# Last keys by pair of visits or one by one, the last rows' order of products, and when weights are converted

## The chip, the cores and the metric

The kernel runs on one core of a Trainium2 chip. The metric is device time in microseconds from start to end of one launch; a kernel's time is the median over its runs. The engines of the core are TensorE (PE; its weight loads are PEld), VectorE (DVE), ScalarE (ACT), GpSimd (POOL) and SyncE (SP), which issues nearly all DMAs.

## The reference

Attention with normalized queries and keys, then a feed-forward network with a squared ReLU. Eight batches, 12 heads, 448 rows, head size 64; the network takes 3584 rows of 768, with 2048 hidden columns.

```python
q_n, k_n = (rmsnorm(q, g_q), rmsnorm(k, g_k))
scores = scale * np.matmul(q_n, k_n.transpose(0, 1, 3, 2))
attn = np.exp(scores - np.max(scores, axis=-1, keepdims=True))
attn = attn / (np.sum(attn, axis=-1, keepdims=True) + 1e-09)
x = np.matmul(attn, v)             # (B,H,S,D), then to (B*S, H*D)
h = np.maximum(x @ w_in, 0.0)
out = h * h @ w_out
```

q, k and v are float32; w_in and w_out come as 64-bit floats and are made into float32 on the chip.

## The kernel before

**Pairs and visits.** Two heads make a pair; there are 48 pairs, numbered i, six for each batch. A pair has 448 keys: three tiles of 128 (slots 0, 1, 2) and 64 last keys (slot NJ = 3). The last keys of an even pair and of the odd pair after it share one tile: the even pair's in partitions 0 to 63, the odd one's in 64 to 127 (`key_of`). A visit to pair i computes its scores (L405), takes the exponentials (L413, into tiles wT with 8 buffers), and multiplies the values of pair i - 1 (`attend`, L490), so values come one visit late. The products of the values gather in PSUM bank 4 from batch 2 on. Pairs up to 24 have two visits each, later ones (`whole`) one.

**Units.** The network's rows come in four units of two batches. A unit of `ffn` has four blocks. A block has first products (14 products, `first_products`, L733: half a block's cost) and second products (`second_products`, L785 and L814). Both matrix products are done by a scheme with seven products instead of eight, P1 to P7, whose left and right sides include sums of weight quarters ("forms") and whose results are added into four quarters of an output tile: c11, c12 in an upper row tile, c21, c22 in a lower. Three PSUM banks serve them by "roles": P1, P6 and P7 gather in role 0, P5 and P3 in role 1, P2 and P4 in role 2 in turn, and after each product VectorE adds the bank into the quarters (L855, L831). A product into a bank waits until the addition before it has read the bank.

**Interleaving.** TensorE's stream is written out by a generator with costs. A unit costs 2008, a block 502, a first product 18, a second product 10. `run(until)` emits products until the cost spent reaches a mark, then an attention visit is emitted, then more products. Unit one runs among the visits of pairs 12 to 24, units two and three among the visits of pairs 24 to 47, unit four has none. After each product, `run` also emits a sum of weight forms, the end of a conversion begun before, and a new conversion if its due time (the list `late`) has come.

**Conversion of weights.** Only unit one does it. There are 64 pieces of 128 x 384, 16 per block: four for each of two "in" tiles, then four for each of two "out" tiles. A piece is loaded (L896, L901; three buffers `words`), split by three ScalarE activations (L915 to L917), then joined by three VectorE steps (L928, L948, L952), spread over two due times. After the fourth piece of a tile come four sums of forms, by VectorE and GpSimd in turn (L974), and a store of the tile to DRAM, from which later units load it. Due times are spaced evenly before: sixteen to a block, from half a block on.

**Joint last keys.** From pair 24 on (`joint`), the last keys of an even pair and the odd one after it are multiplied at one time, in the odd visit, by `attend_both`: four products of 64 x 64 (L502). The odd pair's part goes to bank 0, is copied by ScalarE into a spare `words` buffer (L1189), and is added later in `finish` by VectorE (L609), after which GpSimd multiplies with the inverse of the denominators (L610). Other pairs take the other branch, one multiplication by VectorE (L612). Values of last keys lie in `lasts[0]` and `lasts[1]`, whose other 64 partitions are zero; `load_v` loads them (L355). In the joint case it loads both in the even visit, and `lasts[0]` once more in the odd one.

**Denominators.** In even visits `both_denominators` (L542) gives the sums of the two pairs before in bank 0; VectorE and GpSimd invert and spread them (L552 to L565) as tasks between later products.

**The end.** In the last block of the last unit, the rows of a tile are stored (L860) as soon as they are complete, 128 rows of 768 at a time, on SyncE's queue. The last tile (tt = 2) takes its products in SECOND_ORDER, so that P7, which goes into c21 and c22, comes last.

Of the kernel before, what the change touches and what calls it, by code (L numbers as in the profile page):

```python
# [13 lines left out]
F32 = mybir.dt.float32  # L14
# [3 lines left out]
ALU = mybir.AluOpType  # L18
# [3 lines left out]
P = 128  # L22


NJ = 3
# [198 lines left out]
def program(ctx, tc, rows, v, g, wide, ones, moe_w_in, moe_w_out, out, shift):  # L224

    nc = tc.nc

    B, H, S, D = v.shape
# [5 lines left out]
    HALF = DM // 2  # L234
    REST = S % P
    NT = S // P
    NBLK = 4
# [12 lines left out]
    lasts = [const.tile([P, 2, D], F32, name=f"lasts{n}") for n in range(2)]  # L250
# [15 lines left out]
    weights, sums, inverse, rests, xts, forms = {}, {}, {}, {}, {}, {}  # L266
    complete = deque()


# [4 lines left out]
    def whole(i):  # L274
        return i > 2 * 2 * NPAIR

    def joint(i):

        return whole(i - i % 2 + 1) and not shift

    def slots_of(i, n):

        return [m for m in (2 * n, 2 * n + 1) if m < NJ + 1 - i % 2]

    def values_of(i):

        if i % 2:
            return [0, 1, 2] if joint(i) else [NJ, 0, 1, 2]
        return [0, 1, 2, NJ]

    def key_of(i, m):
        return (i - i % 2, m) if m == NJ and not shift else (i, m)
# [51 lines left out]
    def load_v(i):  # L344
        b, c = pairs[i]
        values[i] = io.tile([P, NJ, 2, D], F32, name="vt", tag="vt")
        for e in range(2):
            nc.sync.dma_start(
                values[i][:, :, e],
                rows.in_chunks(i, v[b, 2 * c + e, 0 : NJ * P]),  # L350
            )
        for odd in range(2):
            if joint(i) != (i % 2 == odd) or joint(i) and i % 2 == 0:
                h = 2 * (c - i % 2 + odd)
                nc.sync.dma_start(  # L355
                    lasts[odd][ds(odd * D, D)],
                    v[b, h : h + 2, NJ * P : S].rearrange("h p d -> p h d"),
                )

    def rescale(i, x):  # L360
        rows.power(i, x)
# [63 lines left out]
    def add_up(i, e, m):  # L425
        if m == 1:
            sums[i, e] = new_sum(i)
            left = weights[(i, 0), e]
        else:
            left = sums[i, e]  # L430
        some = ds(i % 2 * LASTS, LASTS) if m == NJ else ds(0, P)
        nc.gpsimd.tensor_tensor(  # L432
            out=sums[i, e][some], in0=left[some], in1=weights[key_of(i, m), e][some], op=ALU.add
        )
        if joint(i) and i % 2 and m == NJ:
            del weights[key_of(i, m), e]

    def new_sum(i):

# [34 lines left out]
    def values_bank(i):  # L474
        return banks[4 + i % 2 if alone(i) else 4][:, 0:S]

    def attend(i, some):

        order = values_of(i)
        for n in some:
            m = order[n]
            if joint(i) and m == NJ:
                attend_both(i)
                continue
            mine = ds(i % 2 * LASTS, LASTS) if m == NJ and shift else ds(0, P)
            for e in range(2):
                nc.tensor.matmul(  # L490
                    values_bank(i)[ds(e * D, D), :],
                    lhsT=lasts[i % 2][mine, e, :] if m == NJ else values[i][:, m, e, :],
                    rhs=weights[key_of(i, m), e][mine], start=n == 0, stop=n == len(order) - 1,
                )

    def attend_both(i):

        other = banks[0][:, 0:S]
        for p in (i, i + 1):
            r = ds(p % 2 * LASTS, LASTS)  # L500
            for e in range(2):
                nc.tensor.matmul(  # L502
                    (other if p % 2 else values_bank(i))[ds(e * D, D), :],
                    lhsT=lasts[p % 2][r, e, :], rhs=weights[(i, NJ), e][r],
                    start=p > i, stop=True,
                )
        rests[i + 1] = new_words().bitcast(F32).rearrange("p n w -> p (n w)")[:, 0:S]

    def add_weights(i, some):

# [84 lines left out]
    def new_words():  # L595
        return ffn_p.tile([P, HALF, 2], U32, name="words", tag="words", bufs=3)
# [4 lines left out]
    def new_x():  # L601
        return ffn_p.tile([P, S], F32, name="xT", tag="xT", bufs=11 * NK - 1)

    def finish(i):

        b, c = pairs[i]
        xT = xts[b, c] = new_x()
        if joint(i):
            nc.vector.tensor_tensor(out=xT, in0=values_bank(i), in1=rests.pop(i), op=ALU.add)  # L609
            nc.gpsimd.tensor_tensor(out=xT, in0=xT, in1=inverse.pop(i), op=ALU.mult)  # L610
        else:
            nc.vector.tensor_tensor(out=xT, in0=values_bank(i), in1=inverse.pop(i), op=ALU.mult)  # L612
        leave(i)

    def leave(i):
# [81 lines left out]

    FIRST_ORDER = ["P1", "P5", "P2", "P6", "P3", "P4", "P7"]
    SECOND_ORDER = ["P1", "P2", "P5", "P6", "P4", "P3", "P7"]
    COST_IN, COST_OUT = 12 * NK // 2, 10  # L700
    COST = NF // 2 * 7 * COST_IN + NBLK * (NT * 7 + 4) * COST_OUT

# [68 lines left out]
    def second_products(u, blk, hid, sums_, accs):  # L771
# [34 lines left out]
        for tt in range(NT):  # L806
            upper_acc, lower_acc = accs[2 * tt], accs[2 * tt + 1]
            c11, c12 = [upper_acc[:, ts(h, HALF)] for h in range(2)]
            c21, c22 = [lower_acc[:, ts(h, HALF)] for h in range(2)]
            for name in SECOND_ORDER:  # L810
                role, first, left, right = PRODUCTS[name]
                ps = roles[role][:, 0:HALF]
                for t in range(2):
                    nc.tensor.matmul(  # L814
                        ps, lhsT=lefts[left][:, t, ts(tt, P)], rhs=w_sb[t][:, OUT.index(right), :],
                        start=first and t == 0, stop=t == 1,
                        skip_group_check=not first,
                    )
                if name == "P1":
                    add_to(c11, ps, blk == 0)  # L820
                elif name == "P5":
                    add_to(c22, ps, blk == 0)
                elif name == "P2":
                    add_to(c11, ps)
                elif name == "P6":
                    add_to(c12, ps, blk == 0)
                elif name == "P4":
                    if blk == 0:
                        nc.scalar.mul(c21, ps, -1.0)
                    else:  # L830
                        nc.vector.tensor_tensor(out=c21, in0=c21, in1=ps, op=ALU.subtract)  # L831
                elif name == "P3":
                    add_to(c12, ps)
                else:
                    add_to(c21, ps)
                    add_to(c22, ps)
                    to_store.append((tt, 1))
                if name == "P3":
                    to_store.append((tt, 0))
                if name in ("P2", "P4") and blk == NBLK - 1:  # L840
                    while to_store:
                        store_rows(*to_store.popleft())
                yield COST_OUT
            turn_roles(2, 0, 1)
# [6 lines left out]
    def add_to(acc, ps, first=False):  # L851
        if first:
            nc.scalar.copy(acc, ps)
        else:
            nc.vector.tensor_tensor(out=acc, in0=acc, in1=ps, op=ALU.add)  # L855
# [124 lines left out]
    def convert():  # L980
# [13 lines left out]
    block, tile_pieces = COST // NBLK, 4  # L994
    ahead = 4 * tile_pieces
    early = deque(2 + 2.4 * n for n in range(ahead + 1))
    every = block / ahead
    late = deque(
        block + 2 + every * (n - 2 * tile_pieces) for n in range(len(all_pieces) - ahead)
    )  # L1000

    load_weights(0)
    load_weights(1)
# [165 lines left out]
    def visit_whole(i):  # L1169
        run_tasks(len(tasks) + len(pool_tasks))  # L1170
        if i <= last and not shift:
            for m in slots_of(i, 0):
                score(i, m)
        if shift:
            attend_all(i - 1)
        else:
            for n in range(len(values_of(i - 1))):
# [100 lines left out]
```

## Time and profile before

| | us |
|---|---|
| median of three runs | 1426.91 |
| the three runs | 1429.25, 1426.91, 1426.72 |
| the profiled execution | 1429.25 |
| its span, first to last instruction | 1427.5 |
| PE busy | 1401.5 |
| DVE busy | 660.0 |
| ACT busy | 597.4 |
| POOL busy | 689.3 |
| first matmul of unit one, two, four (L733) | 137.4, 503.9, 1165.9 |

A matmul of float32 appears as two instructions, which are passes over the same columns. The profile gives each a length that overlaps the next one, so what a matmul costs is the distance from its start to the next start: 0.3755 us for 448 columns and 0.3225 us for 384. Products that use different halves or quarters of the array start a few nanoseconds apart and run at the same time.

### The profile page before, as it was taken

How to read it: one execution, taken by the hardware profiler on the slowest of the kernel's cores; microseconds unless marked ns; L12 is line 12 of the kernel's file. 1: busy time of each engine (PE TensorE's matmuls, PEld its weight loads, DVE VectorE, ACT ScalarE, POOL GpSimd, SP SyncE). 2: the span in 40 equal slices, each digit the busy share in tenths (PEclk: the TensorE clock that was granted, in tenths of full speed). 3: DMA queues.
4: the chain of work that ended last, by engine and by line, in shares of the span. 5: the costliest groups of instructions: out<-in, count | busy, mean ns of one | idle time of the engine just before them, and what ended most of it. 6: DMA issues, size and time to landing. Idle time of an engine off the chain costs nothing.

```text
span 1427.5 us, 15477 instructions
## 1 busy us (share of the span) xinstructions
PE 1401.5 (98%) x4932; PEld 677.4 (47%) x4932; DVE 660.0 (46%) x1233; ACT 597.4 (42%) x1126; POOL 689.3 (48%) x688
## 2 busy tenths in 40 slices
PE   7999999999999999999999999999999999999998
PEld 3333444444444445445454544445444455555554
DVE  5997365886777623324252453224233251132413
ACT  6874466647555254342424334442432303212130
POOL 5666654655556657356455566365462422021111
PEclk9999999999999999999999999999999999999999
DMA  5765336565667573453435454343622242213122
GB/s 139 195 193 151 67 96 196 157 197 164 197 183 218 160 209 94 127 138 99 138 78 172 122 182 126 74 149 87 185 71 89 95 153 79 111 55 127 39 89 80
DMA packets 311007, 188.51 MB, mean 132 GB/s; under 512 B 267524, under 2 KB 295044, under 8 KB 302724
## 3 DMA queue, kind: packets, MB, share of 16 engines
q1 hardware_dynamic: 310624, 187.36, 44.9%
q8 instruction: 41, 0.67, 0.2%
q14 instruction: 50, 0.41, 0.1%
q10 hardware_dynamic: 292, 0.07, 0.0%
HBM read 144.97 MB, written 42.40 MB: 131 GB/s over the span
## 4 chain that ended last, share of the span: by engine, by line
PE 91%; DVE 4%; issue 1%; SPq 1%; POOL 1%; ACT 1%; DMA 1%; DVEq 0%; POOLq 0%; ACTq 0%
PE bank L733 35%; PE bank L814 29%; PE bank L405 9%; PE bank L490 9%; PE bank L785 5%; PE bank L516 1%; PE bank L502 1%; PE bank L533 1%; PE bank L542 1%; SPq L157 1%; DVE acc L855 0%; DVE out_sb L974 0%; PE bank L370 0%; DVE out_sb L952 0%; DMA qk<-in_q_dram 0%
## 5 line engine op out<-in xcount | busy, mean ns | idle before, releaser
L733 PE MATMUL bank<-xT,in_sb 128*128 128x448 f32 x1344 | 515.4, 542 | 0.0
L733 PEld LDWEIGHTS bank<-xT,in_sb 128*128 128x128 f32 x1344 | 252.4, 190 | 260.4 <-issue 250.5
L855 DVE TENSOR_TENSOR acc<-acc,bank 128x384 f32<-128x384 f32 x324 | 173.8, 550 | 232.9 <-PE bank L814 183.7
L814 PE MATMUL bank<-out_sb,hid 128*128 128x384 f32 x768 | 266.6, 487 | 1.6 <-DVE acc L855 1.6
L753 DVE TENSOR_TENSOR hid<-bank,part 128x448 f32<-128x448 f32 x128 | 76.9, 622 | 331.9 <-PE bank L733 331.6
L413 ACT ACTIVATE wT<-bank,rr 128x448 f32<-128x448 f32 x288 | 161.5, 631 | 116.5 <-PE bank L405 85.2
L814 PE MATMUL bank<-out_sb,sums 128*128 128x384 f32 x576 | 204.0, 490 | 3.4 <-DVE acc L855 3.3
L814 PEld LDWEIGHTS bank<-out_sb,hid 128*128 128x128 f32 x768 | 145.4, 190 | 105.6 <-DVE acc L855 3.6
L202 POOL TENSOR_TENSOR rr<-ms,minus_half 128x8 f32<-128x8 f32 (+1 forms) x96 | 146.2, 1523 | 81.1 <-DVE ms L195 69.7
L769 POOL TENSOR_TENSOR sums<-hid 128x384 f32<-128x384 f32 x32 | 32.2, 1007 | 295.7 <-ACT hid L755 295.7
L405 PE MATMUL bank<-qT,kT 64*128 64x448 f32 (+1 forms) x768 | 164.5, 575 | 1.4 <-DVE qT L378 1.1
L754 ACT ACTIVATE hid<-hid 128x448 f32<-128x448 f32 x128 | 73.3, 572 | 197.1 <-DVE hid L753 197.1
L814 PEld LDWEIGHTS bank<-out_sb,sums 128*128 128x128 f32 x576 | 107.7, 190 | 88.2 <-DVE acc L855 8.4
L740 ACT COPY part<-bank 128x448 f32<-128x448 f32 x128 | 67.7, 529 | 170.9 <-PE bank L733 170.9
L432 POOL TENSOR_TENSOR sum<-sum,wT 128x448 f32<-128x448 f32 (+1 forms) x96 | 110.6, 1173 | 10.9 <-ACT wT L413 8.1
L405 PEld LDWEIGHTS bank<-qT,kT 64*128 64x128 f32 (+1 forms) x768 | 55.5, 174 | 104.6 <-issue 76.9
L490 PE MATMUL bank<-wT,vt 128*64 128x448 f32 x480 | 102.8, 549 | 0.0
L785 PE MATMUL bank<-out_sb,hid 128*128 128x384 f32 x256 | 85.6, 488 | 0.0
L432 POOL TENSOR_TENSOR sum<-wT 128x448 f32<-128x448 f32 x48 | 56.7, 1199 | 49.2 <-ACT wT L413 49.2
L554 POOL COPY few<-few 32x14 f32<-32x14 f32 x48 | 9.0, 188 | 144.9 <-DVE few L552 142.9
L192 DVE TENSOR_REDUCE ms<-squares 128x8 f32<-128x512 f32 (+1 forms) x68 | 41.8, 615 | 77.3 <-ACT squares L179 77.3
L755 ACT ACTIVATE hid<-hid 128x448 f32<-128x448 f32 x128 | 73.8, 577 | 4.1
(101 smaller groups left out, 1287.7 us busy)
## 6 DMA issues: line engine op xcount, KB each, us to landing
out_sb<-out_forms SPq DMA_DIRECT2D x24, 1536.0 KB, 9.4
in_sb<-in_forms SPq DMA_DIRECT2D x24, 1344.0 KB, 5.9
words<-in_moe_w_in_dram SPq DMA_DIRECT2D x32, 384.0 KB, 4.0
words<-in_moe_w_out_dram SPq DMA_DIRECT2D x32, 384.0 KB, 3.8
out_forms<-out_sb SPq DMA_DIRECT2D x8, 1536.0 KB, 7.1
in_forms<-in_sb SPq DMA_DIRECT2D x8, 1344.0 KB, 5.9
qk<-in_q_dram SPq DMA_DIRECT2D x96, 96.0 KB, 3.2
qk<-in_k_dram SPq DMA_DIRECT2D x96, 96.0 KB, 2.7
```

The lines of the kernel that those rows point to most:

```text
L202: self.nc.gpsimd.tensor_tensor(out=self.rr[i][:, x, 0 : self.count(i)], in0=ms, in1=self.minus_half.to_broadcast(list(ms.shape)), op=ALU.pow,)
L405: nc.tensor.matmul(sc[some], lhsT=turned[p, 1][r, keys], rhs=turned[p, 0][r, :], start=True, stop=True,)
L413: nc.scalar.activation(new_weights((i, m), e), sc, AF.Exp, scale=rows.rr[i][:, 1, 2 * m + e : 2 * m + e + 1],)
L432: nc.gpsimd.tensor_tensor(out=sums[i, e][some], in0=left[some], in1=weights[key_of(i, m), e][some], op=ALU.add)
L490: nc.tensor.matmul(values_bank(i)[ds(e * D, D), :], lhsT=lasts[i % 2][mine, e, :] if m == NJ else values[i][:, m, e, :], rhs=weights[key_o ...
L733: nc.tensor.matmul(ps, lhsT=w_sb[:, IN.index(left), c, :], rhs=forms[u, c][right], start=first and c == 0, stop=c == NK - 1, skip_group_ch ...
L753: nc.vector.tensor_tensor(out=dst, in0=left, in1=right, op=op)
L754: nc.scalar.activation(dst, dst, AF.Relu)
L755: nc.scalar.activation(dst, dst, AF.Square)
L785: nc.tensor.matmul(ps, lhsT=flat[a][:, t, ds(NT * P, P)], rhs=w_sb[t][:, 2 * a + half, :], start=(a, t) == parts[0], stop=(a, t) == parts[-1],
L814: nc.tensor.matmul(ps, lhsT=lefts[left][:, t, ts(tt, P)], rhs=w_sb[t][:, OUT.index(right), :], start=first and t == 0, stop=t == 1, skip_g ...
L855: nc.vector.tensor_tensor(out=acc, in0=acc, in1=ps, op=ALU.add)
```

## The change

It has three parts.

1. The joint product of the last keys goes, with its copy, its spare buffer, and its addition. Every pair's last keys are multiplied with the pair's other values, 128 partitions deep (the other half of `lasts` is zero): last in an even pair, first in an odd pair. `load_v` loads the pair's own last values only.
2. In the last row tile of the last block of the last unit, the products come in a new order, P1, P2, P6, P5, P7, P4, P3. The upper row tile is stored by halves: c11 after P2, c12 after P3; the lower one after P4.
3. The due times of the conversions change: of sixteen to a block, eight come 0.06 of a block apart from 0.4 on, and eight 0.055 apart from the start of the next block on.

```diff
     def values_of(i):
 
-        if i % 2:
-            return [0, 1, 2] if joint(i) else [NJ, 0, 1, 2]
-        return [0, 1, 2, NJ]
+        return [NJ, 0, 1, 2] if i % 2 else [0, 1, 2, NJ]
...
-        for odd in range(2):
-            if joint(i) != (i % 2 == odd) or joint(i) and i % 2 == 0:
-                h = 2 * (c - i % 2 + odd)
-                nc.sync.dma_start(
-                    lasts[odd][ds(odd * D, D)],
-                    v[b, h : h + 2, NJ * P : S].rearrange("h p d -> p h d"),
-                )
+        mine = ds(i % 2 * D, D)
+        nc.sync.dma_start(
+            lasts[i % 2][mine],
+            v[b, 2 * c : 2 * c + 2, NJ * P : S].rearrange("h p d -> p h d"),
+        )
...
-            if joint(i) and m == NJ:
-                attend_both(i)
-                continue
...
-        if joint(i):
-            nc.vector.tensor_tensor(out=xT, in0=values_bank(i), in1=rests.pop(i), op=ALU.add)
-            nc.gpsimd.tensor_tensor(out=xT, in0=xT, in1=inverse.pop(i), op=ALU.mult)
-        else:
-            nc.vector.tensor_tensor(out=xT, in0=values_bank(i), in1=inverse.pop(i), op=ALU.mult)
+        nc.vector.tensor_tensor(
+            out=xts[b, c], in0=values_bank(i), in1=inverse.pop(i), op=ALU.mult
+        )
...
     SECOND_ORDER = ["P1", "P2", "P5", "P6", "P4", "P3", "P7"]
+    LAST_ORDER = ["P1", "P2", "P6", "P5", "P7", "P4", "P3"]
...
+                if ends and name == "P4":
                     to_store.append((tt, 1))
-                if name == "P3":
-                    to_store.append((tt, 0))
+                if ends and name in ("P2", "P3"):
+                    half = int(name == "P3")
+                    nc.sync.dma_start(
+                        out[ds(2 * u * S + P * tt, P), ts(half, HALF)], [c11, c12][half]
+                    )
...
-    every = block / ahead
-    late = deque(
-        block + 2 + every * (n - 2 * tile_pieces) for n in range(len(all_pieces) - ahead)
-    )
+    def when(n):
+        step, n = divmod(n, ahead)
+        if n < ahead // 2:
+            return block * (step + 0.4 + 0.06 * n)
+        return block * (step + 1 + 0.055 * (n - ahead // 2)) + 2
+
+    late = deque(when(n) for n in range(len(all_pieces) - ahead))
...
-                nc.scalar.copy(rests[i], banks[0][:, 0:S])
                 xts[pairs[i - 1]] = new_x()
```

Here `ahead` is 16 and `block` is 502; `ends` is true in the last row tile of the last block of the last unit alone.

More of the change, by code (lines that the diff above doesn't have):

```diff
@@ L265, in program @@
     values, turned, through = {}, {}, {}
-    weights, sums, inverse, rests, xts, forms = {}, {}, {}, {}, {}, {}
+    weights, sums, inverse, xts, forms = {}, {}, {}, {}, {}
     complete = deque()
@@ L275, in whole @@
         return i > 2 * 2 * NPAIR
-    def joint(i):
-        return whole(i - i % 2 + 1) and not shift
     def slots_of(i, n):
@@ L434, in add_up @@
         )
-        if joint(i) and i % 2 and m == NJ:
-            del weights[key_of(i, m), e]
     def new_sum(i):
@@ L492, in attend @@
                     lhsT=lasts[i % 2][mine, e, :] if m == NJ else values[i][:, m, e, :],
-                    rhs=weights[key_of(i, m), e][mine], start=n == 0, stop=n == len(order) - 1,
+                    rhs=weights[key_of(i, m), e][mine], start=n == 0, stop=n == NJ,
                 )
[L496 to L505, printed above, removed]
-                )
-        rests[i + 1] = new_words().bitcast(F32).rearrange("p n w -> p (n w)")[:, 0:S]
     def add_weights(i, some):
@@ L606, in finish @@
         b, c = pairs[i]
-        xT = xts[b, c] = new_x()
-        if joint(i):
-            nc.vector.tensor_tensor(out=xT, in0=values_bank(i), in1=rests.pop(i), op=ALU.add)
-            nc.gpsimd.tensor_tensor(out=xT, in0=xT, in1=inverse.pop(i), op=ALU.mult)
-        else:
-            nc.vector.tensor_tensor(out=xT, in0=values_bank(i), in1=inverse.pop(i), op=ALU.mult)
+        xts[b, c] = new_x()
+        nc.vector.tensor_tensor(
+            out=xts[b, c], in0=values_bank(i), in1=inverse.pop(i), op=ALU.mult
+        )
         leave(i)
@@ L809, in second_products @@
             c21, c22 = [lower_acc[:, ts(h, HALF)] for h in range(2)]
-            for name in SECOND_ORDER:
+            ends = final and blk == NBLK - 1 and tt == NT - 1
+            for name in LAST_ORDER if ends else SECOND_ORDER:
                 role, first, left, right = PRODUCTS[name]
@@ L836, in second_products @@
                     add_to(c22, ps)
-                    to_store.append((tt, 1))
-                if name == "P3":
-                    to_store.append((tt, 0))
+                    if not ends:
+                        to_store.append((tt, 1))
+                if name == "P3" and not ends:
+                    to_store.append((tt, 0))
+                if ends and name == "P4":
+                    to_store.append((tt, 1))
+                if ends and name in ("P2", "P3"):
[3 more added lines that the diff above has]
+                    )
                 if name in ("P2", "P4") and blk == NBLK - 1:
@@ L996, in program @@
     early = deque(2 + 2.4 * n for n in range(ahead + 1))
-    every = block / ahead
-    late = deque(
-        block + 2 + every * (n - 2 * tile_pieces) for n in range(len(all_pieces) - ahead)
-    )
+    def when(n):
[4 more added lines that the diff above has]
+    late = deque(when(n) for n in range(len(all_pieces) - ahead))
     load_weights(0)
@@ L1176, in visit_whole @@
         else:
-            for n in range(len(values_of(i - 1))):
+            for n in range(NJ + 1):
                 attend(i - 1, (n,))
```

## The prediction

> **What bounds the kernel.** I first read the page's busy shares, to see whether one engine sets the time.
>
> ```profile
> span 1427.5 us, 15477 instructions
> ...
> PE 1401.5 (98%) x4932; PEld 677.4 (47%) x4932; DVE 660.0 (46%) x1233; ACT 597.4 (42%) x1126; POOL 689.3 (48%) x688
> ```
>
> TensorE does, and the page's row of granted clocks is at its top digit in all 40 slices. So an edit costs what it adds to TensorE's stream or to a gap in it; work on another engine counts only where TensorE waits for it. I then read the stretches of each weight block, one row each: the first unit's four second-product stages start at 185.6, 274.0, 366.2 and 456.1 us. Columns: length, then busy time of PE, PEld, DVE, ACT, POOL.
>
> ```profile
> 185.60:228.80 43.20, 43.20 (x150) 21.95 (x148) 27.68 (x50) 24.75 (x52) 24.88 (x21) 1.00 0.55 144
> ...
> 274.00:321.30 47.30, 45.66 (x159) 22.26 (x157) 40.26 (x71) 21.12 (x41) 29.70 (x24) 1.00 0.67 192
> ...
> 366.20:411.70 45.50, 43.82 (x151) 21.80 (x149) 36.88 (x68) 18.69 (x38) 27.03 (x23) 1.00 0.66 183
> ```
>
> The second and third have PE idle (1.64 and 1.68 us) with VectorE busy for 85% and 81%. From unit two on, rows of this kind show no idle PE but for one stage (793.4 to 840.7 us). Third, the order of time inside one odd attention visit of unit two, PE alone (start, length, line).
>
> ```profile
> 554.39 1.77 PE L405 MATMUL bank<-qT,kT 64*128 64x448 f32 x8
> 556.10 2.48 PE L490 MATMUL bank<-wT,vt 128*64 128x448 f32 x12
> 558.50 0.98 PE L502 MATMUL bank<-wT,lasts 64*64 64x448 f32 x8
> 559.42 1.02 PE L405 MATMUL bank<-qT,kT 64*128 64x448 f32 x4
> ```
>
> L502 is the joint product for the last keys of both pairs. Its 8 instructions use four 64x64 quarters at once and hold TensorE from 558.50 to 559.42: 0.92 us. The even visit after it (581.21) has L405 and L490 in the same places and the denominators' L542, 0.9 us, where L502 stands here.
>
> **Part one, the joint product goes.** The last keys return to L490's form, 4 instructions (two heads, two passes) in each of the two visits. L490's 12 instructions run two at a time: the start distances inside the group are 0.376 us a pair, after a first one of 0.42. One more key group is two such pairs, 0.752 us.
> Even visits (12, the last one at 1141.8): +0.752 each, 9.02 us.
> Odd visits (12): L502 and its change of mode go. Starts now: sixth L490 pair +0.47 to L502, +0.92 to L405. After: 0.376 + 0.376 + 0.469 (the L490 to L405 change, as at 469.6 us). That is 1.22 against 1.38 us, -0.16. In the first odd visit (497.4) the exponentials are late, at +3.87 instead of +2.71, and the score after them starts with them; I count no gain there. 11 x 0.16 = -1.76 us.
>
> On this, the Trainium skill's page TensorEngine Tiling (Array Packing), Theoretical Speedup, speaks against the change: two dimensions of at most 64 give up to twice each. By it the joint group should take two passes, 0.75 us, so that odd visits get nothing back and its loss costs 12 x 0.752 = 9.0 us in all. The page's Key Properties add that a change of tiling mode drains the array; the row's 0.92 us holds that already, so the row decides.
>
> Off TensorE: ScalarE loses 12 copies (L1189, 532 ns each) and GpSimd 12 multiplications (L610, 1138 ns); VectorE's L609 addition (584 ns) becomes the multiplication of L612 (0.61 us). SyncE issues 6 loads of values in two visits instead of 7 (L348, L355), used a visit (27 us) later, so a load that lands in 2.4 us is covered. None of this is on TensorE's path but in one place:
>
> ```profile
> 827.49 2.62 DVE L638 TENSOR_TENSOR xT<-xT 128x448 f32<-128x448 f32 x1 [0.56 <-POOL xT L610]
> 830.03 1.01 DVE L855 TENSOR_TENSOR acc<-acc,bank 128x384 f32<-128x384 f32 x2
> ...
> 830.63 0.59 PE L814 MATMUL bank<-out_sb,hid 128*128 128x384 f32 x1 [1.63 <-DVE acc L855]
> ```
>
> VectorE waits 0.56 us for L610, then adds late, and TensorE waits 1.63 us. Without L610 at least 0.56 goes, at most the 1.63; the subtraction L638 still stands in front of the addition, with 2.62 us here (another at 824.97 takes 1.50), so I take 0.6.
> A weight tile (8 buffers) now stays until the even visit's first product, so there the first two exponentials (now at +1.1 us) wait as they do in odd visits (+2.71, released by L490). Queued behind them on ScalarE are the next two, the last ending at 4.79; the next score starts at 5.75, so 1 us of cover. In odd visits the exponential of the bank ends at 4.27 and the score comes at 4.86: 0.6 us of cover. Where it failed, in the first odd visit, the two heads' scores start 0.151 us apart (502.826 and 502.977) instead of 0.007.
> Sum of part one: 9.02 - 1.76 - 0.6 = **+6.7** (from +5.6, the whole stall at 830 gone, to +7.3).
>
> **Part two, the end.** Here I read the last instructions. The last busy one of all:
>
> ```profile
> 1421.33 1.02 DVE L855 TENSOR_TENSOR acc<-acc,bank 128x384 f32<-128x384 f32 x2 [0.73 <-PE bank L814]
> ```
>
> SyncE issues its last store at 1422.38, as that pair ends. The products keep their number (0.3225 us an instruction). One VectorE addition instead of two stands before the last store, 0.47 us earlier. Its transfer is halved: 384 KB moved in about 1.5 us (its packets, 1422.9 to 1424.5), so up to 0.75 more if the end waited for it. SyncE's next waits come at 1426.11, 3.3 us after its branch at 1422.76; VectorE, which stores nothing, needs the same from its branch (1421.35) to its next instruction (1424.46). So the landing (1425.4) is covered by that. Its packets of instructions (1424.47 and 1425.05) come right behind the store's, so a little more than 0.47 may come with a shorter store: I take -0.6, between -0.4 and -1.3 (0.47 + 0.75). The new order must not stall: P6 now follows P1 after one product, 1.29 us; P1's addition ends 1.08 us after the last P1 instruction starts, and P6 starts 1.61 us after it. The two whole stores of the row group before (384 KB each, now issued at 1411.60 and 1413.35) come to stand behind the first half's on SyncE's queue, which waits for P2's addition (1415.44): some 4 us later, and each moves in 1.5 us, so they are through before the last two.
>
> The Trainium skill's page DMA: Bandwidth & Descriptors (Anatomy of one DMA, for GpSimd's path) has 2.0 us plus bytes over 436e3. Halving would give 0.45 us by it, and part two would be -0.9; the rows say that the end waits for the branch.
>
> **Part three, the pieces of the weights.** Only unit one converts. I worked out the emission order from the costs. Before: 8 pieces at 0 to 0.44 of a block, 8 at 0.5 to 0.94. After: 0 to 0.385 and 0.4 to 0.82. So two pieces move from the second-product stages, where VectorE is full, into the first-product stages (DVE 29.88 of 45.2 us, ACT 32.35). What stalls there now:
>
> ```profile
> 278.90 0.54 DVE L855 TENSOR_TENSOR acc<-acc,bank 128x384 f32<-128x384 f32 x1
> 279.36 1.46 DVE L974 TENSOR_TENSOR out_sb<-out_sb 128x384 f32<-128x384 f32 x1
> 280.75 1.15 DVE L928 TENSOR_SCALAR in_sb<-words 128x384 uint32<-128x384 uint32 x1
> 281.82 0.54 DVE L855 TENSOR_TENSOR acc<-acc,bank 128x384 f32<-128x384 f32 x1
> ...
> 285.22 1.56 PE L814 MATMUL bank<-out_sb,sums 128*128 128x384 f32 x4 [1.25 <-DVE acc L855]
> ```
>
> Between two additions that TensorE waits for stand a weight sum and a conversion, then two more conversion steps. Start distances over the normal pitch at 282.41, 285.22, 374.76 and 377.44 us: 0.55 + 1.41 + 0.73 + 1.28 = 3.97 us. After, these sums come a step earlier and nothing stands between those two additions; but until P7 of the first row group about as many VectorE steps come as before (17 against 18). So most of the 3.97 goes, not all: two thirds, **-2.7** (likely -1.6 to -4). Ends: everything by which unit one's stages exceed the best of their kind, 7.1 us (distances between starts over the normal pitch, summed by stage: 2.93, 3.22, 2.75, 2.45 for first products and 1.91, 4.35, 4.12, 2.79 for second), or +1.5, one more stall as long as the longest above, since in the first-product stages ScalarE's 32.35 us of 45.2 grow by two pieces of three steps (0.56 each), 3.4 us.
>
> **Sum**: 6.7 - 0.6 - 2.7 = +3.4 us. Profiled span 1427.5 becomes 1430.9; that execution took 1429.25 (1.75 around the span) and would take 1432.65; it is the slowest of three. Against the median, 1426.91 + 3.4 = **1430.3**.
>
> **Rivals.** (a) The stalls only move: VectorE's total work in unit one is the same, 17 steps stand where 18 stood. For it: 85% busy. Against it: the long gap between two additions goes. Part three 0, +6.1: 1433.0.
> (b) Not slower: the moved pieces free unit one of all its over-pitch time, -7.1, where part three decides from -6.1 on: 6.7 - 0.6 - 7.1 = -1.0, 1425.9. For it: the stages at 185.6 and 411.7 run at 1.91 and 2.45. Against it: two of the eight sums hold only changes of mode and start waits.
> (c) The exponentials' cover fails, as at 497.4: 11 odd visits lose their gain and 0.15 us each, the split named above: 1.76 + 1.65 = +3.4 more, 1433.7. Against it: ScalarE loses 12 copies, and 11 odd visits of 12 look the same to 0.01 us.
>
> **Chances.** Forecast 0.58 (its own range 1429.0 to 1431.4, part three from -4 to -1.6), (a) 0.20, (b) 0.12, (c) 0.10. Range 1427.4 to 1434.0: it takes in (a), (c) and half of the way to (b). A change of 0.2% (2.85 us) is about what can be told here: above 1429.8 lie (a), (c) and two thirds of the forecast, 0.68; below 1424.1 only (b) overshooting, 0.05; between, 0.27.
>
> **What would show it.** L490 at 16 instructions and visits of 5.82 and 7.65 us (now 5.98 and 6.90); L814's wait for L855 near 283 and 376 us gone or under 0.5; the wait at 830.6 down from 1.63 to about 1.0; the end 0.6 us nearer to the last matmul. It is wrong if visits keep their length, or if unit one (137.4 to 503.9) shrinks by more than 6 us or grows.

## The result, and the profile after

| | before | after |
|---|---|---|
| median of three runs, us | 1426.91 (1426.72 to 1429.25) | 1435.85 (1435.37 to 1437.80) |
| profiled run, us | 1429.25 | 1435.37 |
| its span, us | 1427.5 | 1433.6 |
| start of unit one's products, us | 137.4 | 134.1 |
| unit one | 366.5 | 370.8 |
| units two and three, to the first product after them | 661.9 | 668.0 |
| last matmul's start to end of span | 6.64 | 5.71 |

The ratio of the times is 1.0061 [1.0038, 1.0084]: the change costs 0.6%. The predicted time was 1430.3, in a range up to 1434.0. The two profiled runs are an unlucky pair, the slowest of three before and the fastest of three after, so that their spans differ by 6.1 us where the medians differ by 8.9. The row on unit one's start holds 3.3 us of this, and the last section says where most of them come from.

First the busy shares of the profile after.

```profile
span 1433.6 us, 15416 instructions
...
PE 1405.6 (98%) x4932; PEld 681.1 (48%) x4932; DVE 653.5 (46%) x1233; ACT 591.5 (41%) x1114; POOL 672.6 (47%) x676
```

VectorE, ScalarE and GpSimd have less to do than before, TensorE 4.1 us more. Shares do not show where the rest went; stages do. These are unit one's stages from the second on, one row each, second and first products in turn. The columns are those of the rows in the prediction: length, busy time of the five engines, then the granted clock, the share of the DMA engines and GB/s.

```profile
183.20:226.40 43.20, 43.20 (x150) 21.95 (x148) 26.19 (x45) 21.67 (x46) 25.65 (x22) 1.00 0.68 187
226.40:271.80 45.40, 44.85 (x143) 19.11 (x141) 30.29 (x52) 33.20 (x67) 23.33 (x19) 1.00 0.50 137
271.80:317.70 45.90, 44.63 (x158) 22.01 (x156) 38.78 (x69) 19.96 (x39) 29.16 (x24) 1.00 0.75 220
317.70:365.40 47.70, 44.80 (x142) 19.08 (x140) 34.43 (x59) 36.11 (x72) 25.14 (x21) 1.00 0.51 142
365.40:410.60 45.20, 45.20 (x151) 22.69 (x149) 32.99 (x62) 15.89 (x32) 26.00 (x23) 0.96 0.73 215
410.60:457.60 47.00, 44.88 (x143) 19.12 (x141) 28.99 (x52) 31.09 (x62) 23.30 (x19) 1.00 0.52 148
```

These are the same first-product stages in the kernel before:

```profile
228.80:274.00 45.20, 44.47 (x142) 19.11 (x140) 29.88 (x50) 32.35 (x65) 23.86 (x19) 1.00 0.54 159
321.30:366.20 44.90, 44.77 (x143) 19.04 (x141) 32.23 (x53) 33.33 (x65) 25.47 (x21) 1.00 0.58 175
411.70:456.10 44.40, 44.40 (x143) 19.08 (x141) 29.91 (x50) 31.01 (x62) 23.57 (x19) 1.00 0.68 207
```

The four first-product stages (the first, not shown, has 49.1 us after and 48.2 before) take 189.2 us instead of 182.7: +6.5. In them TensorE's idle time, length less busy, grows from 1.0 to 6.6 us. The four second-product stages (the last has 47.3) take 181.6 instead of 183.8: -2.2; there idle time falls from 3.4 to 1.4 us, and one row (365.4) has a granted clock of 0.96. Sum: +4.3. The list of TensorE's waits in unit one names what is late now (columns: total, number, longest).

```profile
PE bank L397 <- ACT qT L335: 5.0, 4, 2.9
PE bank L507 <- ACT wT L405: 1.6, 1, 1.6
PE bank L788 <- DVE acc L837: 1.3, 2, 1.1
```

The same list before:

```profile
PE bank L814 <- DVE acc L855: 3.3, 4, 1.2
PE bank L533 <- ACT wT L413: 0.7, 1, 0.7
```

It was four waits for VectorE's additions, 3.3 us in all, and one of 0.7 us for an exponential. The additions gave most of theirs back. In their place stand waits of attention visits for **ScalarE**, for the scaled queries (L335, before L341) and the exponentials (L405, before L413). The longest, TensorE and then ScalarE:

```profile
359.73 1.92 PE L397 MATMUL bank<-qT,kT 64*128 64x448 f32 x8
364.55 0.97 PE L397 MATMUL bank<-qT,kT 64*64 64x448 f32 x4 [2.90 <-ACT qT L335]
```

```profile
359.78 0.57 ACT L897 ACTIVATE words<-words 128x384 f32<-128x384 f32 x1 [2.31 <-DMA words<-in_moe_w_in_dram]
360.24 0.54 ACT L898 ACTIVATE words<-words 128x384 f32<-128x384 uint32 x1
360.81 0.58 ACT L899 ACTIVATE words<-words 128x384 uint32<-128x384 f32 x1
361.68 0.58 ACT L727 ACTIVATE hid<-hid 128x448 f32<-128x448 f32 x1 [0.28 <-DVE hid L726]
...
363.84 0.65 ACT L335 ACTIVATE qT<-qT,g 128x448 f32<-128x448 f32 x1
```

An even pair's visit ends with the last keys' scores, which need the next pair's queries as well. ScalarE scales those only at 363.84, behind the three steps of a converted piece, behind the 2.31 us that this piece waited for its load, and behind the four steps on `hid`. That is 4.11 us after the visit's first score. At the same visit of the kernel before it is 1.34 us, and TensorE waits 0.13 us:

```profile
363.24 3.02 PE L405 MATMUL bank<-qT,kT 64*128 64x448 f32 x12
364.58 0.65 ACT L341 ACTIVATE qT<-qT,g 128x448 f32<-128x448 f32 x1
```

Units two and three went as forecast. In the odd visit of unit two:

```profile
556.12 1.77 PE L397 MATMUL bank<-qT,kT 64*128 64x448 f32 x8
557.82 2.48 PE L477 MATMUL bank<-wT,vt 128*64 128x448 f32 x12
560.13 0.92 PE L477 MATMUL bank<-wT,lasts 128*64 128x448 f32 x4
560.98 1.02 PE L397 MATMUL bank<-qT,kT 64*128 64x448 f32 x4
```

L477 now has 16 instructions, and the L397 score starts 4.86 us after the visit's start instead of 5.02. An odd visit takes 5.81 us (was 5.98), an even one 7.65 (was 6.90). The stall in the second unit, near 830 before, is smaller:

```profile
834.14 1.56 PE L788 MATMUL bank<-out_sb,hid 128*128 128x384 f32 x4 [0.47 <-DVE acc L837]
```

### The profile page after: what moved, and what is told of

It reads as the page before. It is cut to its first block, busy times and chain, and to the rows that moved or that the text cites. A ratio compares the mean times of both kernels' runs of the same rounds, so it can differ in the third digit from the quotient of the medians.

```text
span 1433.6 us, 15416 instructions
## 1 busy us (share of the span) xinstructions
PE 1405.6 (98%) x4932; PEld 681.1 (48%) x4932; DVE 653.5 (46%) x1233; ACT 591.5 (41%) x1114; POOL 672.6 (47%) x676
## 4 chain that ended last, share of the span: by engine, by line
PE 90%; ACT 3%; DVE 3%; issue 1%; SPq 1%; POOL 1%; DMA 0%; DVEq 0%; POOLq 0%; ACTq 0%
PE bank L706 34%; PE bank L788 29%; PE bank L477 10%; PE bank L397 9%; PE bank L758 6%; PE bank L490 1%; PE bank L516 1%; ACT wT L405 1%; PE bank L362 1%; PE bank L507 1%; SPq L157 1%; ACT hid L728 1%; ACT hid L727 0%; DVE acc L837 0%; DVE hid L726 0%
## 5 line engine op out<-in xcount | busy, mean ns | idle before, releaser
L405 ACT ACTIVATE wT<-bank,rr 128x448 f32<-128x448 f32 x288 | 160.8, 632 | 133.0 <-PE bank L397 95.9
L397 PE MATMUL bank<-qT,kT 64*128 64x448 f32 (+1 forms) x768 | 164.0, 573 | 6.3 <-ACT qT L335 5.0
L397 PEld LDWEIGHTS bank<-qT,kT 64*128 64x128 f32 (+1 forms) x768 | 55.3, 173 | 108.6 <-issue 68.4
L477 PE MATMUL bank<-wT,vt 128*64 128x448 f32 x480 | 102.2, 546 | 0.0
```

The source lines that it names most:

```text
L397: nc.tensor.matmul(sc[some], lhsT=turned[p, 1][r, keys], rhs=turned[p, 0][r, :], start=True, stop=True,)
L405: nc.scalar.activation(new_weights((i, m), e), sc, AF.Exp, scale=rows.rr[i][:, 1, 2 * m + e : 2 * m + e + 1],)
L477: nc.tensor.matmul(values_bank(i)[ds(e * D, D), :], lhsT=lasts[i % 2][mine, e, :] if m == NJ else values[i][:, m, e, :], rhs=weights[key_o ...
```

## The experiments

Times are medians of 5 to 11 runs. Each was taken beside the kernel before on the same chip; there were three chips, with before at 1426.92, 1427.02 and 1426.95 us. A ratio is to that "before".

### One part at a time

Part one alone (the kernel after, with the old due times of the pieces and the old end):

> The first part alone (last keys one by one), order of the last rows and due times as before. Theory T (each part costs by its own place: the visits +6.1 us, the end -0.9 us, unit one +4.3 us through ScalarE's queue): units two and three longer by 6.1 us, odd visits 5.81 us and even ones 7.65 us, unit one as before (366.5 us), so +6.1 us in all. Rival (the parts act on each other, the exponentials of the visits or the start being disturbed): unit one or the stage at 793 us also change, the sum lies off 6.1 by over 1.5 us.

Measured: 1433.29, ratio 1.0041 [1.0028, 1.0054]; unit one 365.6 us, units two and three 668.0 us (+6.1), as theory T has it.

Part two alone (the kernel before, with `LAST_ORDER` and the halved store):

> The second part alone (new order of products in the last rows, upper rows stored by halves). Theory T: nothing before the last row tile changes, the last matmul comes at the same place, and from it to the end are 5.7 us instead of 6.6: -0.9 us. Rival (the end waits for the branch alone, so only the 0.47 us of the second addition go): -0.5 us, and SyncE's time from its branch to its next wait stays at 3.3 us.

Measured: 1427.01, ratio 0.9993 [0.9984, 1.0002]. The interval holds no change; the 0.9 us that the trace gives is inside it.

Part three alone (the kernel before, with the new `when`):

> The third part alone (new due times of the conversions). Theory T (three conversion steps on ScalarE now stand ahead of the scaling of the queries and of the exponentials, which TensorE waits for): unit one about 371 us instead of 366.5, the first-product stages together 6 us longer, the second-product stages 2 us shorter, +4 us in all. Rival (unit one's length differs from run to run by that much and the due times do nothing): unit one within 1 us of 366.5, time as before within 1 us. The prediction's own view: -2.7 us.

Measured: 1430.85, ratio 1.0025 [1.0016, 1.0034], unit one 369.0 us. The three ratios less 1 add up to 0.0059, the whole change has 0.0061 with an interval of 0.0023 to each side: no dependence of the parts on each other shows. So part three, which was to give 2.7 us, costs 3.9 (1430.85 - 1426.92), and by the same medians no other part is off by more than 0.7. It has the waits of the kernel after:

```profile
PE bank L405 <- ACT qT L341: 5.0, 4, 2.9
PE bank L533 <- ACT wT L413: 1.7, 1, 1.7
PE bank L814 <- DVE acc L855: 1.2, 2, 1.0
```

A small one shows the way in full. ScalarE before one visit, in the kernel with part three alone, and then the same place in the kernel before:

```profile
243.30 0.54 ACT L915 ACTIVATE words<-words 128x384 f32<-128x384 f32 x1
243.75 0.55 ACT L916 ACTIVATE words<-words 128x384 f32<-128x384 uint32 x1
244.33 0.56 ACT L917 ACTIVATE words<-words 128x384 uint32<-128x384 f32 x1
244.79 0.65 ACT L341 ACTIVATE qT<-qT,g 128x448 f32<-128x448 f32 x1
```

```profile
242.84 0.58 ACT L755 ACTIVATE hid<-hid 128x448 f32<-128x448 f32 x1
243.84 0.67 ACT L341 ACTIVATE qT<-qT,g 128x448 f32<-128x448 f32 x1 [0.43 <-DVE qT L339]
```

Without the piece ScalarE waits 0.43 us for the transposed queries. With it, L341 starts only when the third step of the piece is through, 0.95 us later, and TensorE waits 0.55 us at 245.50.

### The in pieces in the second-product stages

The eight in pieces of a block come later than before, from 0.56 of a block on, so that none stands in the first products; the out pieces keep their times of before (edit to the kernel before):

```
+        if n < ahead // 2:
+            return block * (step + 0.56 + 0.055 * n)
+        return block * (step + 1 + (n - ahead // 2) / ahead) + 2
```

> Other due times: the out pieces as before, the eight in pieces from 0.56 of a block on, 0.055 apart, so that they begin after the first additions of the second products and none moves into the first products. Theory T: the stalls at 282 to 286 and 374 to 378 us go as they did in the changed kernel (-2 us in the second-product stages) and the first-product stages keep their length: -2 us. Rival (VectorE's work in the second products is too much wherever it stands, the stalls only move): unit one within 1 us of 366.5, no gain.

Measured: 1437.22, ratio 1.0064 [1.0050, 1.0078], unit one 374.4 us. Both expectations missed.

```profile
PE bank L814 <- DVE acc L855: 5.6, 5, 1.5
PE bank L533 <- ACT wT L413: 4.5, 3, 2.2
PE bank L405 <- ACT qT L341: 1.5, 2, 0.9
```

The pieces crowd VectorE late in the stage, and the store of the input forms goes out in the next first-product stage, at 244.23. A store of queries issued behind it lands only after 7.96 us, SyncE waits for that until 253.40 and then issues twelve loads of queries and keys, and so a load of words that itself takes 3.49 us is issued only at 260.39. ScalarE stands 6.79 us before its L915 at 263.97, with the exponentials (L413, 266.55) queued behind it, and TensorE waits 2.25 us at 268.88. A piece that waits for its load stops all that ScalarE has behind it.

### Only the out pieces moved

Part three, with the in pieces at their times of before:

```
-            return block * (step + 0.4 + 0.06 * n)
+            return block * (step + 0.5 + n / ahead) + 2
```

> Of the new due times only the out pieces' (0.055 of a block apart); the in pieces as before. Theory T: the two in pieces that had moved into the first products are back, so the waits at 185 and 367 us fall to the 0.13 us of before (-3.6 us against the third part alone); those at 246, 428 and 450 us (0.55, 0.55, 1.7), which the out pieces' times make, stay; unit one 366 to 367.5 us. Rival O (the closer spacing of the out pieces makes all five waits): unit one 369 us.

Measured: 1427.61, ratio 1.0006 [0.9996, 1.0016]. Of part three's 3.9 us, 3.3 go with the in pieces' new times, by which two pieces had moved (3.93 - 0.59, medians, both against before on their chip). The profiled run is the slowest of its eleven (1431.59, granted clock 0.995), with 368.6 us in unit one. Its waits at the visits near 185 and 364 us are down to 0.13 us and those near 245 and 425 us keep 0.55 us, as expected; one exponential (448.68, 2.73 us) became later.

### Scaling the queries on VectorE

Part three, with one more edit:

```
-            nc.scalar.mul(dst, dst, g)
+            nc.vector.tensor_scalar(out=dst, in0=dst, scalar1=g, scalar2=None, op0=ALU.mult)
```

> The third part alone, and the scaling of the transposed queries (L341) by VectorE in place of ScalarE. Theory T (in unit one conversion steps now stand in ScalarE's and VectorE's queues ahead of what the last keys' scores wait for): the two waits at 246 and 428 us, where ScalarE's three steps stand right before the scaling, go (0.55 us each), those at 185 and 367 us, where VectorE and a landing are late too, shrink by 0.4 to 0.5 us; unit one 367 us instead of 369.0. Rival V (all four waits come from VectorE's queue): nothing shrinks by more than 0.3 us, and unit one keeps 369 us or grows.

Measured: 1434.06, ratio 1.0047 [1.0034, 1.0061], unit one 373.7 us. The waits near 246 and 428 us went, as expected: there ScalarE's three steps ahead of the scaling were the cause. Those near 185 and 367 fell only from 1.04 to 0.82 and from 2.88 to 2.68: there ScalarE's `hid` steps and VectorE's conversions are late as a chain, wherever the scaling stands. VectorE, one step fuller, then kept TensorE waiting 2.54 us for an addition at 280.73, and the exponentials were 3.14 us late at 452. The place of the step was right and the total missed. By the trace most of the miss is clock: TensorE's waits in unit one sum to 9.1 us against 7.9 with part three alone, but behind three of them the granted clock was 0.79 over 8 us (from 280.7, 366.7 and 452.0; 8 x 0.21 = 1.7 us each), where part three alone kept 1.00 all through unit one. The last section comes back to this.

### Stores of the forms only in second products

Part three, with the stores kept out of the first-product stages. The suspicion was that they delay the load that ScalarE waits for:

```
+    def make_sum(store=True):
...
+        elif forms_to_store and store:
...
+            make_sum(store=cost != COST_IN)
```

> The third part alone, and the stores of converted tiles (1.3 and 1.5 MB) are issued in second products only. Theory D (the longest waits, 2.88 us at 367 and 1.66 us at 450, begin with a piece whose load lands late, 5 to 6.5 us after its issue, because a transfer of 1.5 MB is ahead of it, and ScalarE waits 2.3 to 2.5 us for it): the one at 367 falls to about 0.6 us and unit one to 366.5 us; the one at 450, behind a load of forms, stays. Rival (the steps' own 1.7 us on ScalarE and 1.5 us on VectorE make them): both keep over 1.4 us, unit one 369 us.

Measured: 1435.87, ratio 1.0052 [1.0039, 1.0066], unit one 374.8 us. ScalarE's wait for that load fell from 2.25 to 0.70 us (364.33), and TensorE's wait after it stayed at 2.89 us. VectorE in that stretch shows why:

```profile
363.24 0.69 DVE L192 TENSOR_REDUCE ms<-squares 128x8 f32<-128x512 f32 x1 [2.21 <-ACT squares L179]
...
364.61 0.52 DVE L974 TENSOR_TENSOR out_sb<-out_sb 128x384 f32<-128x384 f32 x1
365.05 0.55 DVE L948 SCALAR_TENSOR_TENSOR in_sb<-words,in_sb 128x384 uint32<-128x384 uint32 x1
365.63 0.56 DVE L952 CUSTOM_DVE_ANT_0 in_sb<-words,in_sb 128x768 uint16<-128x768 uint16 x1
366.11 1.16 DVE L928 TENSOR_SCALAR in_sb<-words 128x384 uint32<-128x384 uint32 x1
367.18 1.14 DVE L753 TENSOR_TENSOR hid<-bank,part 128x448 f32<-128x448 f32 x2
...
369.30 0.64 DVE L339 STREAM_TRANSPOSE qT<-qk 128x448 f32<-128x448 f32 x1
```

A weight sum and the join of two pieces stand ahead of the additions that make `hid` (L753) and of the queries' transpose (L339), and VectorE itself waited 2.21 us for squares that ScalarE computes behind another piece. The late landing alone is not the cause. The two engines wait for each other in turn, with the pieces between. What makes this kernel slower than part three alone shows in its trace as one more wait for an addition (1.98 us at 303.38) and as a granted clock of 0.79 over the 8 us behind it and behind the 2.89 us wait.

### More pieces, or pieces at the wrong place?

Two explanations were left: one more pair of pieces is too much for a first-product stage, or the pieces stand at the wrong place in it. This kernel has the schedule of before with as many conversions, in the same stages; six out pieces come one first product later (18 units of cost).

```
+    def when(n):
+        due = block + 2 + every * (n - 2 * tile_pieces)
+        return due + COST_IN * (ahead // 2 <= n % ahead < ahead - 2)
```

> The kernel before, with six of the eight out pieces due one first product (18 of cost) later: the same number of conversions in every stage, but four of them now in the product right before an attention visit (before: none of the eight). Theory T (what costs is a conversion step in the queues of VectorE and ScalarE right ahead of a visit's queries and exponentials): new waits of 0.5 us and more at visits of the first products, which lengthen by 2 to 6 us together; unit one 368 to 372 us. Rival N (what costs is the number of conversion steps in the first products): first-product stages within 0.7 us of before, no change of time beyond 1 us.

Measured: 1436.56, ratio 1.0070 [1.0055, 1.0086], unit one 374.8 us. One number in the expectation needs putting right: of the six, two come right ahead of a visit and two ahead of its half-way mark, not four ahead of visits. The new waits are at those two visits of the second and the fourth block: 0.66 us at 241.95 and 426.81 (the first of the two), 2.24 us at 264.69 and the one below (the second).

```profile
447.00 0.55 ACT L915 ACTIVATE words<-words 128x384 f32<-128x384 f32 x1 [5.79 <-DMA words<-in_moe_w_out_dram]
447.45 0.53 ACT L916 ACTIVATE words<-words 128x384 f32<-128x384 uint32 x1
448.02 0.54 ACT L917 ACTIVATE words<-words 128x384 uint32<-128x384 f32 x1
448.46 2.19 ACT L413 ACTIVATE wT<-bank,rr 128x448 f32<-128x448 f32 x4
```

```profile
450.80 0.97 PE L533 MATMUL bank<-sum,ones 128*64 128x448 f32 x4 [3.48 <-ACT wT L413]
```

With the number of pieces in each stage as before, a shift of six of them by one product costs 9.6 us, as much as the whole change and more than was expected (the fastest of its six runs, at a granted clock of 0.999, has +7.0). The place alone is enough. It acts through SyncE's queue as well: the load that ScalarE waits for here was issued at 440.60, behind a load of forms (439.95), and took 6.37 us; in the kernel before it was issued at 438.44, ahead of that one (439.06), and took 3.54.

### Smaller stores, and the multiplication on VectorE

The kernel before with part two, and with each converted tile's store issued as four, each once its part is ready:

```
-        forms_to_store.append(((in_forms if kind == "in" else out_forms)[t], dst))
+        for n in range(0, dst.shape[1], 2):
+            some = ds(n, min(2, dst.shape[1] - n))
+            forms_to_store.append((to[:, some], dst[:, some]))
```

> The kernel before with the second part (new order and halves at the end), and each converted tile stored by four transfers, one after each product, in place of one of 1.3 or 1.5 MB. Theory D: what waits on SyncE's queue and in the transfers behind a store (queries' round trip, 6 to 8 us; pieces' loads, 5 to 6.5 us) comes earlier, ScalarE waits less for pieces, and the waits at 266 and 285 and 376 us (0.9, 1.25, 0.95) shrink: unit one 364.5 to 366 us, the end -0.9 us, 1 to 3 us faster than before. Rival (only the landing is earlier and nobody on TensorE's path gains): the end's -0.9 us alone.

Measured: 1424.52 (1423.02 to 1425.36 in eleven runs), ratio 0.9980 [0.9971, 0.9989]: **faster than both kernels**, by 0.2% against before. The reason given for it fell all the same: unit one takes 367.3 us, no less than before. Units two and three keep their 661.9 us, so the gain beyond part two (5.84 us from the last matmul to the end instead of 6.64) comes ahead of unit one. In the kernel before SyncE waits 4.0 us there for the sums that its one store of 1536 KB needs, with the loads of values queued behind it, and issues the load of the last values from 106.91 us; with four stores it does so from 104.90. TensorE's wait for them:

```profile
109.34 1.76 PE L490 MATMUL bank<-wT,lasts 128*64 128x448 f32 x4 [2.45 <-DVE xT L612]
```

```profile
107.80 0.97 PE L490 MATMUL bank<-wT,lasts 128*64 128x448 f32 x4 [0.93 <-DMA lasts<-in_v_dram]
```

The first line is of the kernel before, the second of this one. (The releaser that the first line names is the last by the profile; in six other profiles the same wait is put down to the load of the last values.) The next kernel has the same stores and 0.94 us there; the ten other profiles of this study have 2.3 to 2.7.

That next kernel has L610's multiplication on VectorE too, to take away the wait for GpSimd near 830 us:

> The kernel before with the new end and the stores in parts, as in the run before, and the joint pairs' multiplication (L610) by VectorE in place of GpSimd. Theory (the wait of 1.63 us at 830 us comes from GpSimd: VectorE waits 0.56 us for L610 and its subtraction L638 takes 2.6 us beside GpSimd's): that wait falls to about 0.5 us, as in the changed kernel, nothing else moves, -1 us against the stores in parts alone. Rival (VectorE's own addition and multiplication come as late): the wait keeps over 1.3 us, no gain.

Measured: 1425.86, ratio 0.9987 [0.9978, 0.9997]. The wait fell from 1.63 to 0.72 us; the time does not differ from the kernel without the edit by more than the intervals allow, so the 1 us expected does not show.

## Why the prediction was wrong

The direction was right and the time 1.9 us above the range's upper end. By its own steps:

- **Part one, +6.7.** Measured +6.1 in the trace, both in the whole change and alone. Even visits +0.75 and odd ones -0.16 came as worked out, with nothing in the first odd one. The stall at 830 was taken to lose 0.6 and lost 1.16 (1.63 to 0.47), which is the difference. The row's 0.92 us for the joint group held: had it been two passes of 0.376 us, odd visits would have kept their length.
- **Part two, -0.6.** The trace shows -0.9 between the last matmul and the end. The other profiles with the old end have 6.61 to 6.67 us there, and once 7.40; those with the new end 5.52 to 5.84. SyncE's branch to its next wait fell from 3.35 to 2.73 us (3.32 to 3.36 in all profiles with the old end, 2.71 to 2.89 with the new). So the branch's time changed with the end of the kernel, by 0.62 us, where the prediction allowed 0.13 beyond the addition's 0.47; what shortened it was not tried. The estimate of -0.9 from the Trainium skill's page DMA: Bandwidth & Descriptors (Anatomy of one DMA, for GpSimd's path) agrees with the trace better than the term taken from the rows. It agrees in the total alone: the halved store landed no sooner after its issue (3.64 us, from 1428.97, against 3.02 from 1422.38). In the times, the part alone is not told from nothing.
- **Part three, -2.7: this is the step that failed.** "these sums come a step earlier and nothing stands between those two additions" was right: idle time in the second-product stages fell from 3.4 to 1.4 us. What failed was the cost of the same move. The sum has no term for it; it stands only as an end of the range: "or +1.5, one more stall as long as the longest above, since in the first-product stages ScalarE's 32.35 us of 45.2 grow by two pieces of three steps". That weighed 3.4 us more work against the room in a stage, and left the likely cost at nothing. But ScalarE ran its steps in the order in which they were emitted (L915 to L917, then L341 at 244.79), and the new times put pieces right ahead of visits. The emission order, worked out from the costs for the number of pieces, would have told it: in block one, counted from zero, visits come after the first products at 592, 682 and 754 units of cost. The conversions of before begin at 574, 610, 664, 700 and so on, never straight ahead of one; after, some begin at 592 and 682, and a further piece with a weight sum stands ahead of 754. The waits of part three alone lie at these places of their blocks, though not at every one: near 245 and 428 (after 592), 450 (after 682), 184 and 367 us (after 754). With them the first-product stages grew by 6.5 us; less the gain of the second-product stages, unit one grew by 4.3 us in the whole change, and part three alone cost 3.9, where -2.7 was forecast and +1.5 was the worst allowed for. With +3.9 in its place the prediction's sum gives 1436.9.
- **Rivals.** (a), "the stalls only move" (1433.0), came nearest in kind; (c) lies nearer in time, 1433.7, by a way that did not come. (a) had the stalls go from one addition to another on VectorE; they went to ScalarE, to another stage, and became more. (b) and (c) did not come: the exponentials' cover in units two and three held, with eleven odd visits of 5.81 us.
- **The marks.** That unit one "grows" had been named as what would make the prediction wrong, and it did, from 366.5 to 370.8 us. The other marks came (16 instructions, both visits, a shorter wait near 830, a nearer end), but for one: of the addition's waits, that near 376 us went, and 1.08 us were left of that near 283 (at 279.56), where at most 0.5 was named.

What stays open: which of the pieces' steps ahead of the visit at 754 sets the wait there. Less waiting for the load and scaling on VectorE each left 2.7 to 2.9 us of it.

## What to carry to other kernels

Where a step is moved on an engine that works in order, ask first what stands behind it, and when the critical engine needs that; idle time of a stage says nothing about it. Lay the emission order of before and after beside the points at which the critical engine consumes something, and look for steps that have come to stand straight ahead of one, above all steps that can wait for a load. A store that waits in a queue for its data delays the loads behind it in the same manner: issued in parts, and with the new end, the kernel gained 0.2%, a good part of it because TensorE kept its clock (next section).

## What the runs showed of the hardware

After a wait of some 2 us or more TensorE often ran at half its clock for 3 to 6 us. In the kernel before, the stretch behind the 2.45 us wait at 109.34, and in the kernel with the shifted pieces, the stretch behind the 3.48 us wait (the granted clock is the third number from the end):

```profile
109.30:114.00 4.70, 4.66 (x12) 1.39 (x12) 4.54 (x9) 1.87 (x4) 2.50 (x2) 0.50 1.04 283
```

```profile
450.80:456.00 5.20, 5.20 (x11) 2.41 (x12) 3.74 (x9) 3.67 (x9) 2.82 (x3) 0.67 0.24 82
```

In the kernel after, the 7.9 us behind the 2.90 us wait at 364.55 have 0.78: second products start 0.64 us apart there instead of 0.3225, until the clock is back. That is 7.9 x 0.22 = 1.7 us, and why its stage at 365.4 gained only 0.3. Part three alone had the same wait (2.88 us) at full clock, and a unit one shorter by 1.8 us. In the twelve profiles, 22 waits between 100 us and the end were of 1.9 us or longer, and behind 15 of them the starts lay twice as far apart; behind the 40 waits of 0.9 to 1.7 us, none did. In the traces' record of the granted clock 11 of these 15 stretches last 3.41 us and 4 last 6.83; some begin within the wait, others up to 1.5 us behind it. In the kernel before, the 8.0 us from 109.30 have a clock of 0.62: 8.0 x 0.38 = 3.0 us lost behind a wait of 2.45. So a wait can cost twice its length, and it differs from run to run. The kernel after has a 2.51 us wait at the same place at clock 1.00. From the end of that wait to unit one it takes 25.9 us, the kernel before 28.1, and this is 2.2 of the 3.3 us in the first table.

The runs' times show it too. Of the 61 runs of the kernel before beside the experiments, the 26 with a mean granted clock of 0.999 or more took 1425.8 us on average, the 21 with 0.998 took 1427.4, and the 14 with less took 1428.8. The kernel with smaller stores waits 0.93 us at that place, and all its eleven runs have 0.999 or 1.000 (1424.4 us on average). At equal clock it is ahead by 1.4 us of its 2.5.

The Trainium skill's page TensorE: Matmul & The Clock Gate (Part 1: The HAM clock gate) describes such a gate: half rate after an idle window of about 3.4 us, in windows that run freely, so that the point differs between runs. The halving and its irregular coming agree with the rows here; waits of 1.98 to 3.14 us, shorter than that window, were enough in 14 of the 15 cases.
